# The last chunk's second layer by seven block products, five of them in float32r

## The chip, the cores and the metric

The kernel runs on one core of a Trainium2 chip. The time is that of the device in microseconds (us). An execution that the hardware profiler takes is shown beside the plain runs. The engines work from queues of their own: PE (TensorE, matmuls), DVE (VectorE), ACT (ScalarE), POOL (GpSimd) and SP (SyncE, which issues DMAs). "PEld" is PE's loading of the stationary operand, which a matmul needs first. The product goes into one of eight PSUM banks, from which DVE or ACT read it.

## The reference

Attention for 8 batches, 8 heads, 576 positions and 64 dimensions, with a mask of the last 32 positions for four heads and a mask of every 32nd position for the other four. Its result, 4608 tokens of 512 values, is the input of two layers:

```python
h = x @ w_in                    # 4608 x 512 by 512 x 2048
r = np.maximum(h, 0.0)
g = r * r
return (g @ w_out).astype(np.float32)   # 4608 x 2048 by 2048 x 512
```

## The kernel before

The 4608 tokens are cut into nine chunks of 512. A chunk's first layer (`mm1`, line 731) is 16 groups, one for each block of 128 hidden values: four matmuls of 128x128 weights by 512 tokens into one of two PSUM banks, then relu on ACT into a buffer `r` (four of them, line 745), then the square on DVE into `g` (line 746), one group later. The second layer (`mm2`, line 750) is also 16 groups: for each of the chunk's four blocks of 128 tokens, four groups of four matmuls. In each the stationary operand is a 128x128 block of `g` and the moving one a 128x512 row block of `w_out`; 16 of them add up in one bank. ACT copies the bank out (line 765) and SP issues the store (line 769).

The groups of all chunks stand in one list, numbered from 0: chunk c has its first layer in groups 32c to 32c+15 and its second in 32c+16 to 32c+31. An order written out by hand (`PLAN`) says which steps of the attention come before which group; its last words stand at group 217. `later(n, f)` puts off the issue of f by n groups, and `tick()` after each group issues what is due. So each engine's queue has a fixed order, and only the semaphores decide when an instruction starts. Chunk 7 is groups 224 to 255, chunk 8, the last, 256 to 287. Beside these two chunks nothing but the end of the attention's last steps is left.

The very last block of 128 tokens is cut finer (`last_y`, line 775): 16 matmuls of 256 columns, then 16 and 16 of 128, so that the last copy and the last store are small. The first two parts are copied by ACT, the last by DVE.

All matmul operands are bf16, 2 bytes. Sums in PSUM and the copied outputs are float32. SBUF tiles come from pools that live as long as the kernel.

Of the kernel before, what the change touches and what calls it, by code (L numbers as in the profile page):

```python
# [8 lines left out]
FP32 = mybir.dt.float32  # L9
BF16 = mybir.dt.bfloat16  # L10
AF = mybir.ActivationFunctionType
ALU = mybir.AluOpType
# [155 lines left out]
def kernel(  # L168
# [9 lines left out]
    nc = tc.nc  # L178
    B, H, S, D = q.shape
    d_model, d_ff = moe_w_in.shape  # L180
    T = B * S
# [4 lines left out]
    NL = S // QL  # L186
# [4 lines left out]
    VP = 72  # L191
    SR = 80
    NP2 = STRIDE // 2
    NG = 5
    NB = NP2 + NG + 1
    W3 = 3 * NA
    RW = STRIDE * D
    ER = S + 32

    singles = ctx.enter_context(tc.tile_pool(name="singles", bufs=1))  # L200
    qk_in = ctx.enter_context(tc.tile_pool(name="qk_in", bufs=4))
    qkT = ctx.enter_context(tc.tile_pool(name="qkT", bufs=4))
    v_st = ctx.enter_context(tc.tile_pool(name="v_st", bufs=1))
    rv_pool = ctx.enter_context(tc.tile_pool(name="rv_pool", bufs=3))
    small = ctx.enter_context(tc.tile_pool(name="small", bufs=4))
    xl_pool = ctx.enter_context(tc.tile_pool(name="xl_pool", bufs=4))
    g_pool = ctx.enter_context(tc.tile_pool(name="g_pool", bufs=2))
    r_pool = ctx.enter_context(tc.tile_pool(name="r_pool", bufs=4))
    y_pool = ctx.enter_context(tc.tile_pool(name="y_pool", bufs=4))

    PS = bass.MemoryType.PSUM
    strTs = {nm: ctx.enter_context(tc.tile_pool(name=f"strT{nm}", bufs=n)) for nm, n in (("q", 2), ("k", 1))}
    psum = ctx.enter_context(tc.tile_pool(name="psum", bufs=1, space=PS))
    psb = psum.tile([128, 8, 512], FP32, name="psb")
    all_banks = [psb[:, i] for i in range(8)]
# [4 lines left out]
    def bank(nm):  # L220
        if places:
            return all_banks[places.pop(0)]
        t = banks[nm].pop(0)
        banks[nm].append(t)
        while id(t) in unread:
            run_due(lambda x: x[1] == unread[id(t)])
        return t
# [10 lines left out]
    NV = 4  # L238
# [1 line left out]
    mask_loc = singles.tile([128, 1, QL], BF16)  # L240
    mask_all = singles.tile([128, NL, QL], BF16)
    mask_str = singles.tile([SP_, 1, SP_], BF16)
    vl_all = singles.tile([128, NV, 2, NL, VP], BF16, name="vl")
    vls = [vl_all[:, i] for i in range(NV)]

    vbds = [singles.tile([128, NB, 128], BF16, name=f"vb{i}") for i in range(2)]
    kbds = [singles.tile([128, NB, 128], BF16, name=f"kb{i}") for i in range(2)]
    ones_bd = singles.tile([128, 128], BF16)
    mask_bd = singles.tile([128, 1, W3], BF16)
    str_rows_t = {nm: singles.tile([SR, RW], BF16, name=f"{nm}_t") for nm in "qk"}  # L250
    kTl = [singles.tile([128, 32 + S], BF16, name=f"kTl{i}") for i in range(NV)]
    es01 = singles.tile([128, 4 * ER], BF16, name="e01")
    es = [es01[:, 0:2 * ER], es01[:, 2 * ER:]] + [singles.tile([128, 2 * ER], BF16, name=f"e{i}") for i in (2, 3)]
    xt = [singles.tile([128, T], BF16, name=f"xt{p}") for p in range(4)]
    w_in_b = singles.tile([128, 4, d_ff], BF16)
    w_out_b = singles.tile([128, 16, d_model], BF16)
# [210 lines left out]
    def later(n, fn, key=None):  # L467
        pending.append((clock[0] + n, key, fn))

    def run_due(test):  # L470
        due = [x for x in pending if test(x)]
        for x in due:
            pending.remove(x)
        for x in sorted(due, key=lambda x: x[0]):
            x[2]()

    def tick():
        clock[0] += 1
        run_due(lambda x: x[0] <= clock[0])
# [229 lines left out]
    def step_E(u, copy=None):  # L709
# [14 lines left out]
        copy(xt[p][:, b * S:(b + 1) * S], px)  # L724
        st.pop(u)

    gs = {}

    phs = {}

    def mm1(c, ff, kks=range(4), order=range(4), pool=None):
        if ff == 0 and c not in gs:
            gs[c] = g_pool.tile([128, 16, 512], BF16, name="g_sb")
        g = gs[c]
        if kks[0] == order[0]:
            phs[ff] = bank(pool or "ph")
        ph = phs[ff]
        for kk in kks:
            nc.tensor.matmul(ph, w_in_b[:, kk, 128 * ff:128 * (ff + 1)],  # L739
                             xt[kk][:, 512 * c:512 * (c + 1)],  # L740
                             start=(kk == order[0]), stop=(kk == order[-1]))
        if kks[-1] != order[-1]:
            return
        r = r_pool.tile([128, 512], BF16, name="r")
        nc.scalar.activation(r, ph, AF.Relu)  # L745
        later(1, lambda: nc.vector.tensor_tensor(g[:, ff, :], r, r, op=ALU.mult))  # L746

    ys = {}

    def mm2(c, i, pool=None):  # L750
        j, part = divmod(i, 4)
        g = gs[c]
        if part == 0:
            if pool == "pt":
                ys[c, j] = bank("pt")
                banks["pt"].remove(ys[c, j])
            else:
                ys[c, j] = bank(pool or "py")
        py = ys[c, j]
        for ff in range(4 * part, 4 * part + 4):  # L760
            nc.tensor.matmul(py, g[:, ff, 128 * j:128 * (j + 1)], w_out_b[:, ff, :],  # L761
                             start=(ff == 0), stop=(ff == 15))
        if part == 3:
            y = y_pool.tile([128, 512], FP32, name="y")
            nc.scalar.copy(y, py)  # L765
            if pool == "pt":
                banks["pt"].insert(0, py)
            r0 = 512 * c + 128 * j
            nc.sync.dma_start(out=out[r0:r0 + 128, :], in_=y)

    NCH = T // 512
    A, V, G = nc.scalar.copy, nc.vector.tensor_copy, nc.gpsimd.tensor_copy
    ENG = {"a": A, "v": V, "g": G}

    def last_y(c, j, i):
        g, r0 = gs[c], 512 * c + 128 * j
        if i == 0:
            ys[c, j] = y_pool.tile([128, 512], FP32, name="y")
        y = ys[c, j]
        cols = (slice(0, 256), slice(0, 256), slice(256, 384), slice(384, 512))[i]  # L780
        ffs = (range(0, 8), range(8, 16), range(16), range(16))[i]
        if i != 1:
            ys[c, j, i] = bank("ph")
        py = ys[c, j, 0 if i == 1 else i]
        for ff in ffs:
            nc.tensor.matmul(py[:, cols], g[:, ff, 128 * j:128 * (j + 1)], w_out_b[:, ff, cols],  # L786
                             start=(ff == 0), stop=(ff == 15))
        if i:
            (V if i == 3 else A)(y[:, cols], py[:, cols])
            (nc.scalar if i == 2 else nc.sync).dma_start(out=out[r0:r0 + 128, cols], in_=y[:, cols])  # L790

    def warm(n):
        if n:
# [6 lines left out]
    def first_part(kks, ffs):  # L800
        for ff in ffs:
            mm1(0, ff, kks, FIRST, None if ff < 2 else "py")
# [144 lines left out]
    groups = []  # L947

    def add(c, kind, i, pool=None):
        if kind == 0:  # L950
            groups.append(lambda: None)
        elif kind == 1:
            groups.append(lambda: mm1(c, i, pool=pool))
        elif c == NCH - 1 and i >= 12:
            groups.append(lambda: last_y(c, i // 4, i % 4))
        else:
            groups.append(lambda: mm2(c, i, pool))

    for ff in range(16):
        add(0, 1, ff, {NP: "pt", 8: "py"}.get(ff)) if ff >= NP else add(0, 0, ff)  # L960
    for part in range(4):
        for j, pool in ((0, "ph"), (1, "ph"), (2, None), (3, "pt")):
            add(0, 2, 4 * j + part, pool)
    for i in range(16):
        add(1, 1, i)
    for i in range(16):
        add(1, 2, i, "ph")
    for c in range(2, NCH):
        for i in range(16):
            add(c, 1, i)  # L970
        for i in range(16):
            add(c, 2, i, "ph")

    plan = {}
    for line in PLAN.strip().splitlines():
        n, words = line.split(":")
        plan.setdefault(int(n), []).extend(words.split())
    for n, g in enumerate(groups):
        if n == 32:
            banks["pt"] += banks.pop("py")  # L980
        for word in plan.get(n, ()):
            run_step(word)
        g()
        tick()
    for _ in range(4):
# [31 lines left out]
```

## Time and profile before

| | us |
|---|---|
| plain runs, median of three | 301.57 |
| plain runs | 302.65, 298.83, 301.57 |
| the profiled execution | 299.14 |
| its span, first to last instruction | 297.4 |
| PE busy | 287.8 |
| DVE busy | 180.3 |
| ACT busy | 170.5 |
| POOL busy | 73.3 |

The span is what the trace covers, and the execution's own time is 1.74 us more. Busy times of engines overlap; a matmul's end is modelled and runs into the next one's start, so the pitch of matmuls (start to start) says more than the duration of one. Chunk 7's first layer lies at 238.06 to 251.88 us of the span, its second to 265.69, chunk 8's first to 279.50 and its second to 293.56. What follows is the last copy and the last store.

### The profile page before, as it was taken

What the parts mean: (1) busy time and instruction counts of PE and PEld (TensorE: products, weight loads), DVE (VectorE), ACT (ScalarE), POOL (GpSimd) and SP (SyncE); (2) the same over time, 40 slices, a digit from 0 to 9 for tenths busy, and PEclk for the clock granted to TensorE, in tenths of its full rate; (3) what the DMA queues carried; (4) which work ended last, traced back from release to release, by engine and by line L of the source; (5) the groups of instructions that cost most, each with busy time, mean ns of one, the idle gap of its engine ahead of it and who ended that gap; (6) DMA issues with size and microseconds to landing.
All of it is one profiled execution on the core that took longest, in us unless ns stands there. A gap on an engine that the chain in (4) does not pass through costs nothing.

```text
span 297.4 us, 5621 instructions
## 1 busy us (share of the span) xinstructions
PE 287.8 (97%) x2112; PEld 144.6 (49%) x2148; DVE 180.3 (61%) x465; ACT 170.5 (57%) x318; POOL 73.3 (25%) x107
## 2 busy tenths in 40 slices
PE   7989999999999999999999999999999999999994
PEld 2644555544545454444454445544544444444444
DVE  5557689697777769779367936776575334004300
ACT  3758846774668636764577447744764266127411
POOL 8874743014513036065105700000000000000000
PEclk9999999999999999999999999999999999999999
DMA  7999999999999999999998999411011100020012
GB/s 146 183 207 204 189 199 189 156 224 204 168 179 179 123 164 199 160 144 188 179 128 125 177 149 145 82 55 73 35 31 47 71 37 0 35 89 20 0 71 73
DMA packets 91724, 37.38 MB, mean 126 GB/s; under 512 B 77549, under 2 KB 85831, under 8 KB 91697
## 3 DMA queue, kind: packets, MB, share of 16 engines
q0 software_dynamic: 50608, 18.33, 55.8%
q1 hardware_dynamic: 40944, 18.62, 32.3%
q8 instruction: 17, 0.28, 0.4%
q14 instruction: 11, 0.08, 0.1%
q10 hardware_dynamic: 144, 0.07, 0.1%
HBM read 37.22 MB, written 9.44 MB: 157 GB/s over the span
## 4 chain that ended last, share of the span: by engine, by line
PE 94%; DMA 2%; issue 1%; DVE 1%; ACT 0%; POOL 0%; DVEq 0%; POOLq 0%
PE psb L739 42%; PE psb L761 40%; DMA w_out_b<-in_k_dram 2%; PE psb L699 2%; PE psb L621 1%; PE psb L607 1%; PE psb L786 1%; PE psb L618 1%; PE psb L583 1%; PE psb L538 1%; PE psb L486 1%; DVE xt L668 0%; PE psb L508 0%; PE psb L333 0%; DVE x_l L688 0%
## 5 line engine op out<-in xcount | busy, mean ns | idle before, releaser
L739 PE MATMUL psb<-xt,w_in_b 128*128 128x512 bf16 x558 | 132.1, 379 | 1.2 <-DVE xt L668 0.2
L761 PE MATMUL psb<-w_out_b,g_sb 128*128 128x512 bf16 x542 | 125.3, 379 | 1.2 <-issue 0.5
L745 ACT ACTIVATE r<-psb 128x512 bf16<-128x512 f32 x144 | 85.3, 599 | 37.9 <-PE psb L739 32.8
L746 DVE TENSOR_TENSOR g_sb<-r 128x512 bf16<-128x512 bf16 x144 | 60.4, 423 | 68.5 <-ACT r L745 67.2
L739 PEld LDWEIGHTS <-w_in_b 128*128 128x128 bf16 x576 | 53.2, 97 | 58.9 <-issue 1.4
L761 PEld LDWEIGHTS <-g_sb 128*128 128x128 bf16 x560 | 52.0, 98 | 57.9 <-DVE g_sb L746 0.3
L765 ACT COPY y<-psb 128x512 f32<-128x512 f32 x35 | 20.6, 588 | 51.6 <-PE psb L761 48.6
L631 DVE TENSOR_TENSOR xt<-psb,rv 64x144 bf16<-64x144 f32 x84 | 34.0, 405 | 12.7 <-ACT rv L624 11.6
L623 ACT ACTIVATE rv<-psb 128x432 f32<-128x432 f32 (+1 forms) x21 | 10.5, 501 | 12.8 <-PE psb L618 12.8
L705 DVE TENSOR_TENSOR x_l<-psb,rinv 96x384 bf16<-96x384 f32 x28 | 15.5, 553 | 1.0
L361 POOL DMA_DIRECT2D q_t<-in_q_dram x6 | 3.3, 544 | 45.8 <-DMA qT_s<-q_t 44.9
L594 ACT ACTIVATE e<-psb 128x384 bf16<-128x384 f32 x30 | 12.0, 513 | 4.2 <-PE psb L583 4.2
L608 ACT ACTIVATE e<-psb 128x432 bf16<-128x432 f32 (+1 forms) x21 | 10.4, 496 | 4.0 <-PE psb L607 4.0
L637 DVE TENSOR_TENSOR xt<-psb,rv 64x270 bf16<-64x270 f32 (+1 forms) x28 | 11.0, 433 | 2.5 <-ACT rv L624 2.3
L290 POOL DMA_DIRECT2D q_l<-in_q_dram x16 | 12.0, 754 | 1.6 <-DMA q_l<-in_q_dram 1.4
L290 POOL DMA_DIRECT2D k_l<-in_k_dram x16 | 11.7, 736 | 1.6 <-DMA v_st<-in_v_dram 1.5
L624 ACT ACTIVATE rv<-rv 128x432 f32<-128x432 f32 (+1 forms) x21 | 11.2, 533 | 0.7
L590 DVE TENSOR_TENSOR e<-e,mask_all 128x576 bf16<-128x576 bf16 x20 | 8.4, 456 | 4.9 <-ACT e L594 4.9
L699 PEld LDWEIGHTS <-e 128*128 128x128 bf16 x168 | 8.0, 97 | 4.6
L361 POOL DMA_DIRECT2D k_t<-in_k_dram x6 | 3.2, 536 | 25.0 <-DMA kT_s<-k_t 22.9
L699 PE MATMUL psb<-vl,e 128*128 128x65 bf16 x168 | 9.0, 193 | 0.0
L607 PEld LDWEIGHTS <-kb 128*128 128x128 bf16 x154 | 6.8, 96 | 4.5
(119 smaller groups left out, 213.5 us busy)
## 6 DMA issues: line engine op xcount, KB each, us to landing
out_dram<-y SPq DMA_DIRECT2D x35, 256.0 KB, 4.2
w_out_b<-in_moe_w_out_dram POOLq DMA_DIRECT2D x4, 512.0 KB, 15.1
q_t<-in_q_dram POOLq DMA_DIRECT2D x7, 288.0 KB, 7.3
k_t<-in_k_dram POOLq DMA_DIRECT2D x7, 288.0 KB, 6.9
vl<-in_v_dram POOLq DMA_DIRECT2D x6, 288.0 KB, 7.7
v_st<-in_v_dram POOLq DMA_DIRECT2D x7, 216.0 KB, 6.8
w_in_b<-in_moe_w_in_dram POOLq DMA_DIRECT2D x2, 704.0 KB, 14.3
k_l<-in_k_dram POOLq DMA_DIRECT2D x16, 72.0 KB, 7.0
```

Source lines behind the costliest of these rows:

```text
L290: nc.gpsimd.dma_start(out=t[:, :, hh, :], in_=src[b, 2 * p + hh].rearrange("(t p) d -> p t d", p=QL))
L594: nc.scalar.activation(e[:, row, 4 * QL * i:4 * QL * (i + 1)], bk[row][i][:, 0:4 * QL], AF.Exp, scale=scale)
L624: nc.scalar.activation(rv, rv, AF.Exp, scale=-1.0)
L631: nc.vector.tensor_tensor(to[:, :, NJ * part:NJ * (part + 1), par], of, by, op=ALU.mult)
L637: nc.vector.tensor_tensor(t, of[:, g:, :, lo:lo + k], by[:, g:, :, lo:lo + k], op=ALU.mult)
L699: nc.tensor.matmul(po[:, n, :], e[:, c:c + 128], rhs[:, NL * part + n, 0:D + 1], start=True, stop=True)
L705: nc.vector.tensor_tensor(x, po[0:QL, :, 0:D], rinv[0:QL].to_broadcast([QL, NL, D]), op=ALU.mult)
L739: nc.tensor.matmul(ph, w_in_b[:, kk, 128 * ff:128 * (ff + 1)], xt[kk][:, 512 * c:512 * (c + 1)], start=(kk == order[0]), stop=(kk == order ...
L745: nc.scalar.activation(r, ph, AF.Relu)
L746: later(1, lambda: nc.vector.tensor_tensor(g[:, ff, :], r, r, op=ALU.mult))
L761: nc.tensor.matmul(py, g[:, ff, 128 * j:128 * (j + 1)], w_out_b[:, ff, :], start=(ff == 0), stop=(ff == 15))
L765: nc.scalar.copy(y, py)
```

## The change

The second layer of chunk 8 is written as a product of 2x2 blocks. The 512 tokens are taken as two halves u of 256, each of two blocks of 128 (t = 0, 1); the 2048 hidden values as two halves of 1024 (blocks 0 to 7 and 8 to 15 of `g`); the 512 outputs as two halves of 256 columns. Each half u then needs eight products of such blocks, each of which is eight matmuls of 256 columns. The new code forms seven, in Winograd's way, from sums of blocks of `g` and of `w_out`:

- `weight_sums` forms, in groups 228 to 247, four differences of blocks of `w_out` on DVE (16 subtractions of 128x512, groups 228 to 243) and one copy of a block on ACT (4 copies, groups 244 to 247), all into float32r tiles (4 bytes).
- `squares` takes the place of the squaring in chunk 8. Behind every second squaring DVE forms three sums of 128x256 (S1, S2, S3, where S1 needs the square just made and S2 needs S1), and POOL copies one block, all to float32r; a fourth sum S4 is put off into the second layer. Blocks come in the order 0, 8, 1, 9, ... instead of 0, 1, 2, ...
- `mm2_7` runs the products in the order 1, 2, 6, 7, 4, 5, 3, each for u = 0 and then u = 1: 14 groups of eight matmuls. Products 1 and 2 are of bf16 operands, the other five of float32r ones, whose weights the matmul instruction itself loads. Product 2 adds onto product 1 in PSUM after ACT has copied product 1 out, 7 onto 6 after DVE has read 6, and 3 onto 5 after DVE has read 5. DVE adds PSUM and a tile of SBUF for products 6, 7, 4, 5 and 3; ACT copies for 1 and 2.
- Stores go out after products 5 and 3. Those of the last half: 128x256 early from SP, the rest as two parts of 128x128 behind two DVE adds, one issued by ACT, one by SP.
- `last_y` is gone.
- The attention's tiles are moved to pools that are closed before the new tiles are made, so that these take the same SBUF addresses.

```diff
-    qk_in = ctx.enter_context(tc.tile_pool(name="qk_in", bufs=4))
...
+    att = ctx.enter_context(ExitStack())
+    rows = ctx.enter_context(ExitStack())
...
         nc.scalar.activation(r, ph, AF.Relu)
+        if c in SEVEN:
+            later(1, lambda: squares(c, ff, r))
+            return
         later(1, lambda: nc.vector.tensor_tensor(g[:, ff, :], r, r, op=ALU.mult))
...
+    def weight_sums(step):
...
+        if nm == "b":
+            nc.scalar.copy(t["b"], b22)
+            return
+        x, y = {"1": (b12, b11), "3": (b22, b12), "2": (b22, t["1"]), "4": (b21, t["2"])}[nm]
+        nc.vector.tensor_tensor(t[nm], x, y, op=ALU.subtract)
...
+    def squares(c, ff, r):
...
+        nc.vector.tensor_tensor(g[:, ff, :], r, r, op=ALU.mult)
+        if ff < 8:
+            return
+        S = {k: x[:, i] for k, x in ss.items()}
+        a1, a2 = (g[:, k, :].rearrange("p (u t c) -> p u t c", u=2, t=2) for k in (i, ff))
+        nc.gpsimd.tensor_copy(S["a"], a2[:, :, 1])
+        nc.vector.tensor_tensor(S["1"], a1[:, :, 1], a2[:, :, 1], op=ALU.add)
+        nc.vector.tensor_tensor(S["2"], S["1"], a1[:, :, 0], op=ALU.subtract)
+        nc.vector.tensor_tensor(S["3"], a1[:, :, 0], a1[:, :, 1], op=ALU.subtract)
+        last = lambda: nc.vector.tensor_tensor(S["4"], a2[:, :, 0], S["2"], op=ALU.subtract)
+        later(15 + (1, 2, 3, 4, 6, 7, 8, 9)[i] - 2 * i, last)
...
+    ORDER7 = "1 2 6 7 4 5 3".split()
+
+    def mm2_7(c, i):
+        n, u = ORDER7[i // 2], i % 2
...
+        for k in range(8):
+            a = g[:, k, t0] if n == "1" else g[:, 8 + k, t0] if n == "2" else \
+                ss[{"6": "2", "7": "3", "4": "a", "5": "1", "3": "4"}[n]][:, k, u]
+            b = w_out_b[:, k, lo] if n == "1" else w_out_b[:, 8 + k, lo] if n == "2" else \
+                ts[{"6": "2", "7": "3", "4": "4", "5": "1", "3": "b"}[n]][:, k]
+            nc.tensor.matmul(pa, a, b, start=k == 0 and n not in "273", stop=k == 7, skip_group_check=True)
+        if n in "12":
+            nc.scalar.copy((y2 if n == "1" else y1)[:, lo], pa)
+            return
...
+        if n == "3" and c == NCH - 1 and u:
+            nc.sync.dma_start(out=out[r0:r0 + 128, lo], in_=y1[:, lo])
+            for h, eng in ((0, nc.scalar), (128, nc.sync)):
+                nc.vector.tensor_tensor(to[:, h:h + 128], pa[:, h:h + 128], by[:, h:h + 128], op=ALU.add)
+                eng.dma_start(out=out[r0:r0 + 128, 256 + h:384 + h], in_=to[:, h:h + 128])
+            return
+        nc.vector.tensor_tensor(to, pa, by, op=ALU.add)
+        if n in "53":
+            r0 += 128 * (n == "5")
+            nc.sync.dma_start(out=out[r0:r0 + 128, :], in_=y2 if n == "5" else y1)
...
-            add(c, 1, i)
+            add(c, 1, i // 2 + 8 * (i % 2) if c in SEVEN else i)
...
+    SUMS = range(228, 248)
...
+        if n in SUMS:
+            weight_sums(SUMS.index(n))
```

More of the change, by code (lines that the diff above doesn't have):

```diff
@@ L200 @@
     singles = ctx.enter_context(tc.tile_pool(name="singles", bufs=1))
-    qk_in = ctx.enter_context(tc.tile_pool(name="qk_in", bufs=4))
-    qkT = ctx.enter_context(tc.tile_pool(name="qkT", bufs=4))
-    v_st = ctx.enter_context(tc.tile_pool(name="v_st", bufs=1))
-    rv_pool = ctx.enter_context(tc.tile_pool(name="rv_pool", bufs=3))
     small = ctx.enter_context(tc.tile_pool(name="small", bufs=4))
-    xl_pool = ctx.enter_context(tc.tile_pool(name="xl_pool", bufs=4))
     g_pool = ctx.enter_context(tc.tile_pool(name="g_pool", bufs=2))
@@ L209 @@
     y_pool = ctx.enter_context(tc.tile_pool(name="y_pool", bufs=4))
+    att = ctx.enter_context(ExitStack())
+    rows = ctx.enter_context(ExitStack())
+    att_singles = att.enter_context(tc.tile_pool(name="att_singles", bufs=1))
+    rv_pool = att.enter_context(tc.tile_pool(name="rv_pool", bufs=3))
+    xl_pool = att.enter_context(tc.tile_pool(name="xl_pool", bufs=4))
+    row_singles = rows.enter_context(tc.tile_pool(name="row_singles", bufs=1, side="right"))
+    qk_in = rows.enter_context(tc.tile_pool(name="qk_in", bufs=4, side="right"))
+    qkT = rows.enter_context(tc.tile_pool(name="qkT", bufs=4, side="right"))
+    v_st = rows.enter_context(tc.tile_pool(name="v_st", bufs=1, side="right"))
     PS = bass.MemoryType.PSUM
-    strTs = {nm: ctx.enter_context(tc.tile_pool(name=f"strT{nm}", bufs=n)) for nm, n in (("q", 2), ("k", 1))}
+    strTs = {nm: rows.enter_context(tc.tile_pool(name=f"strT{nm}", bufs=n, side="right")) for nm, n in (("q", 2), ("k", 1))}
     psum = ctx.enter_context(tc.tile_pool(name="psum", bufs=1, space=PS))
@@ L242 @@
     mask_str = singles.tile([SP_, 1, SP_], BF16)
-    vl_all = singles.tile([128, NV, 2, NL, VP], BF16, name="vl")
+    vl_all = att_singles.tile([128, NV, 2, NL, VP], BF16, name="vl")
     vls = [vl_all[:, i] for i in range(NV)]
-    vbds = [singles.tile([128, NB, 128], BF16, name=f"vb{i}") for i in range(2)]
-    kbds = [singles.tile([128, NB, 128], BF16, name=f"kb{i}") for i in range(2)]
+    vbds = [att_singles.tile([128, NB, 128], BF16, name=f"vb{i}") for i in range(2)]
+    kbds = [row_singles.tile([128, NB, 128], BF16, name=f"kb{i}") for i in range(2)]
     ones_bd = singles.tile([128, 128], BF16)
     mask_bd = singles.tile([128, 1, W3], BF16)
[L250 to L253, printed above, removed]
+    str_rows_t = {nm: row_singles.tile([SR, RW], BF16, name=f"{nm}_t") for nm in "qk"}
+    kTl = [row_singles.tile([128, 32 + S], BF16, name=f"kTl{i}") for i in range(NV)]
+    es01 = att_singles.tile([128, 4 * ER], BF16, name="e01")
+    es = [es01[:, 0:2 * ER], es01[:, 2 * ER:]] + [att_singles.tile([128, 2 * ER], BF16, name=f"e{i}") for i in (2, 3)]
     xt = [singles.tile([128, T], BF16, name=f"xt{p}") for p in range(4)]
@@ L725, in step_E @@
         st.pop(u)
+    NCH = T // 512
     gs = {}
@@ L731, in mm1 @@
     def mm1(c, ff, kks=range(4), order=range(4), pool=None):
-        if ff == 0 and c not in gs:
+        if c not in gs:
             gs[c] = g_pool.tile([128, 16, 512], BF16, name="g_sb")
@@ L745, in mm1 @@
         nc.scalar.activation(r, ph, AF.Relu)
+        if c in SEVEN:
+            later(1, lambda: squares(c, ff, r))
+            return
         later(1, lambda: nc.vector.tensor_tensor(g[:, ff, :], r, r, op=ALU.mult))
+    SEVEN = (NCH - 1,)
+    ts, ss = {}, {}
+    def weight_sums(step):
+        F32R = mybir.dt.float32r
+        if not ts:
+            rows.close()
+            late = ctx.enter_context(tc.tile_pool(name="late", bufs=1, side="right", reuse_waits="tile"))
+            for nm in ("1", "2", "3", "4", "b"):
+                ts[nm] = late.tile([128, 8, 256], F32R, name=f"t{nm}")
+        nm, i = "1234b"[step // 4], 2 * (step % 4)
+        lo, hi = slice(i, i + 2), slice(8 + i, 10 + i)
+        b11, b12 = w_out_b[:, lo, 0:256], w_out_b[:, lo, 256:512]
+        b21, b22 = w_out_b[:, hi, 0:256], w_out_b[:, hi, 256:512]
+        t = {k: x[:, lo] for k, x in ts.items()}
+        if nm == "b":
[3 more added lines that the diff above has]
+        nc.vector.tensor_tensor(t[nm], x, y, op=ALU.subtract)
@@ new lines, in squares @@
+    def squares(c, ff, r):
+        g, i = gs[c], ff % 8
+        if not ss:
+            att.close()
+            late = ctx.enter_context(tc.tile_pool(name="sums", bufs=1, reuse_waits="tile"))
+            for nm in ("1", "2", "3", "4", "a"):
+                ss[nm] = late.tile([128, 8, 2, 128], mybir.dt.float32r, name=f"s{nm}")
+        nc.vector.tensor_tensor(g[:, ff, :], r, r, op=ALU.mult)
[9 more added lines that the diff above has]
+        later(15 + (1, 2, 3, 4, 6, 7, 8, 9)[i] - 2 * i, last)
@@ new lines @@
+    ORDER7 = "1 2 6 7 4 5 3".split()
+    def mm2_7(c, i):
+        n, u = ORDER7[i // 2], i % 2
+        g, r0 = gs[c], 512 * c + 256 * u
+        t0 = slice(256 * u, 256 * u + 128)
+        if n == "1":
+            ys[c, u] = [y_pool.tile([128, 512], FP32, name="y") for _ in range(2)]
+            ys[c, u, "p"] = [bank("pt")]
+        if n == "6":
+            ys[c, u, "p"].append(bank("pt"))
+        y1, y2 = ys[c, u]
+        lo, hi = slice(0, 256), slice(256, 512)
+        pa = ys[c, u, "p"][n not in "124"][:, lo]
+        for k in range(8):
[7 more added lines that the diff above has]
+            return
+        to, by = {"6": (y1[:, hi], y2[:, lo]), "7": (y2[:, hi], y2[:, lo]), "4": (y2[:, lo], y2[:, hi]),
+                  "5": (y2[:, hi], y2[:, hi]), "3": (y1[:, hi], y1[:, hi])}[n]
+        if n == "3" and c == NCH - 1 and u:
[8 more added lines that the diff above has]
+            nc.sync.dma_start(out=out[r0:r0 + 128, :], in_=y2 if n == "5" else y1)
@@ L769, in mm2 @@
             nc.sync.dma_start(out=out[r0:r0 + 128, :], in_=y)
-    NCH = T // 512
     A, V, G = nc.scalar.copy, nc.vector.tensor_copy, nc.gpsimd.tensor_copy
     ENG = {"a": A, "v": V, "g": G}
[L775 to L790, printed above, removed]
     def warm(n):
@@ L953, in add @@
             groups.append(lambda: mm1(c, i, pool=pool))
-        elif c == NCH - 1 and i >= 12:
-            groups.append(lambda: last_y(c, i // 4, i % 4))
+        elif c in SEVEN:
+            groups.append(lambda: mm2_7(c, i) if i < 14 else None)
         else:
```

## The prediction

> **What bounds the kernel now.** I read the engine table first, then the chain that ended last, then a table of time by stage, and then the end of the timeline.
>
> ```profile
> span 297.4 us, 5621 instructions
> ...
> PE 287.8 (97%) x2112; PEld 144.6 (49%) x2148; DVE 180.3 (61%) x465; ACT 170.5 (57%) x318; POOL 73.3 (25%) x107
> ...
> PEclk9999999999999999999999999999999999999999
> ...
> PE 94%; DMA 2%; issue 1%; DVE 1%; ACT 0%; POOL 0%; DVEq 0%; POOLq 0%
> ```
>
> PE is busy for 97% of the span at the full granted clock, and 94% of the last chain is PE. So a change must alter PE's work, or make PE wait. The stage table (columns: stretch, length, then busy time and instruction count of PE, weight loads, VectorE, ScalarE, GpSimd) shows the four stages that matter: first and second layer of chunk 7, then of chunk 8.
>
> ```profile
> 238.06:251.88 13.82, 13.76 (x64) 6.24 (x65) 5.99 (x15) 9.54 (x16) 0.00 (x0) 1.00 0.05 20
> 251.88:265.69 13.81, 13.76 (x64) 6.26 (x64) 0.81 (x2) 2.35 (x4) 0.00 (x0) 1.00 0.15 57
> 265.69:279.50 13.81, 13.76 (x64) 6.26 (x64) 5.98 (x15) 9.54 (x16) 0.00 (x0) 1.00 0.06 21
> 279.50:293.56 14.06, 14.01 (x96) 8.03 (x95) 0.82 (x2) 2.99 (x6) 0.00 (x0) 1.00 0.18 66
> ```
>
> Each full stage is 64 matmuls of 512 columns in 13.81 us, 215.8 ns each, with the weight loads hidden. The changed stage is the last row, 14.06 us. VectorE is under half busy in first layers and nearly idle in second ones; GpSimd is idle. In the listings of both programs every engine's order and waits are the same up to chunk 7, so only these rows and the tail can change; the new pools move addresses alone.
>
> ```profile
> 279.50 10.52 PE L761 MATMUL psb<-w_out_b,g_sb 128*128 128x512 bf16 x47
> 279.70 0.60 ACT L745 ACTIVATE r<-psb 128x512 bf16<-128x512 f32 x1 [0.27 <-PE psb L739]
> 280.33 0.42 DVE L746 TENSOR_TENSOR g_sb<-r 128x512 bf16<-128x512 bf16 x1 [0.44 <-ACT r L745]
> ...
> 289.86 3.70 PE L786 MATMUL psb<-w_out_b,g_sb 128*128 128x256 bf16 x48
> 290.06 0.58 ACT L765 COPY y<-psb 128x512 f32<-128x512 f32 x1 [2.87 <-PE psb L761]
> 291.81 0.37 ACT L789 COPY y<-psb 128x256 f32<-128x256 f32 x1 [1.16 <-PE psb L786]
> ...
> 293.65 0.29 DVE L789 COPY y<-psb 128x128 f32<-128x128 f32 x1 [12.89 <-PE psb L786]
> ```
>
> **Step 1, the matmuls.** Removed: 48 matmuls of 512 columns, 16 of 256, 32 of 128. Added: 7 products x 2 halves x 8 = 112 of 256 columns, 32 of them bf16 and 80 float32r. A reader on ScalarE starts 0.20 us behind the last matmul (289.86, where the next began, to 290.06). So the 16 matmuls of 256 columns end at 291.81 - 0.20 = 291.61: 1.75 us from 289.86, 109 ns each. If all 112 take that, the stage's PE work is 112 x 0.109 = 12.21 us against 14.06: **-1.85 us**.
>
> **Step 2, the price of float32r.** The trace has no such matmul. The lower end is the bf16 pitch, 109 ns. The upper ends come from rows of weight loads and streams:
>
> ```profile
> L786 PEld LDWEIGHTS <-g_sb x48: 97/98/98, 289.6 to 293.3; 128*128 128x128 bf16 x48
> ```
>
> The 32 matmuls of 128 columns take 293.56 - 291.61 = 1.95 us, 61 ns each, each with a bf16 weight load; so such a load occupies the array 61 ns at most. A load of twice the bytes would then take up to 122 ns, more than the 109 it hides under: 80 x 13 ns = 1.04 us. If the load cannot run ahead of the matmul before it, the 98 ns of this row come on top: 207 ns, 80 x 98 ns = +7.8 us. If the moving operand streams by bytes, 256 columns cost as much as 512 of bf16, 216 ns: +8.6 us. Below nothing it cannot go, as the columns are the same. I take the middle of 109 and 122, because the nearest rows are those with hidden loads: **+0.5 us**; the other ends are a rival.
>
> [...] No run here shows a 4-byte load.
>
> **Step 3, weight sums in chunk 7.** Before groups 228 to 243 VectorE gets 16 subtractions of 128x512 with float32r output, 12 of them among the squarings of chunk 7's first layer. Their price needs the engine's pitch, which is less than its duration:
>
> ```profile
> 61.92 0.41 DVE L746 TENSOR_TENSOR g_sb<-r 128x512 bf16<-128x512 bf16 x1
> 62.25 0.35 DVE L309 COPY k_l<-xt 96x768 bf16<-96x768 bf16 x1
> 62.52 0.41 DVE L746 TENSOR_TENSOR g_sb<-r 128x512 bf16<-128x512 bf16 x1
> 62.86 0.18 DVE L704 RECIPROCAL rinv<-psb 96x6 f32<-96x6 f32 x1
> 63.08 0.55 DVE L705 TENSOR_TENSOR x_l<-psb,rinv 96x384 bf16<-96x384 f32 x1
> ```
> ```profile
> L746 DVE TENSOR_TENSOR g_sb<-r 128x512 bf16<-128x512 bf16 x144 | 60.4, 423 | 68.5 <-ACT r L745 67.2
> ...
> L590 DVE TENSOR_TENSOR e<-e,mask_all 128x576 bf16<-128x576 bf16 x20 | 8.4, 456 | 4.9 <-ACT e L594 4.9
> ```
>
> An independent successor starts 0.33 us after a squaring (61.92 to 62.25), though that lasts 0.42; one that needs the result (reciprocal to L705) starts 0.04 us after its end. Squarings of 512 and masks of 576 bf16 differ by 33 ns for 64 elements, 0.52 ns each. The f32-sourced 96x384 takes 0.55 us; at 0.52 ns per element its 384 would take 0.36, so 4-byte elements go at about 1.04 ns. A 128x512 sum with 4-byte output then lasts 0.69 us at a pitch of 0.60 (bounds: 0.42 if the output type does not slow it). With a squaring that is 0.93 us a group, against PE's 13.81 / 16 = 0.863:
>
> ```profile
> 242.35 0.42 DVE L746 TENSOR_TENSOR g_sb<-r 128x512 bf16<-128x512 bf16 x1 [0.44 <-ACT r L745]
> ```
> ```profile
> 252.71 0.42 DVE L746 TENSOR_TENSOR g_sb<-r 128x512 bf16<-128x512 bf16 x1 [0.44 <-ACT r L745]
> ```
>
> Squaring 3 starts at 242.35, the first sum at 242.68, squaring 4 at 243.28 instead of 243.21; each later one loses 0.07 more, so squaring 15 starts near 253.6 instead of 252.71 and ends near 254.0. Its matmul comes at 251.88 + 15 x 0.216 = 255.1. **0 us**, hidden by 1 us. The last four sums and ScalarE's four copies of a weight block lie in the second layer, where both engines are nearly idle (0.81 and 2.35 us of 13.81); without that cover each copy would cost ScalarE's queue its 0.6 us.
>
> **Step 4, sums of the squares in chunk 8.** This is where PE is made to wait. The first layer now runs blocks 0, 8, 1, 9, ...; per pair VectorE does two squarings and three sums of 128x256 with 4-byte output. At 1.04 ns per element such a sum costs as many cycles as a squaring, 0.42 us with a pitch of 0.33.
>
> ```profile
> 267.38 0.42 DVE L746 TENSOR_TENSOR g_sb<-r 128x512 bf16<-128x512 bf16 x1 [14.25 <-ACT r L745]
> ...
> 268.25 0.43 DVE L746 TENSOR_TENSOR g_sb<-r 128x512 bf16<-128x512 bf16 x1 [0.44 <-ACT r L745]
> ```
>
> S1 needs the second squaring and S2 needs S1, so both wait out 0.43 + 0.04. A pair takes 0.33 (first squaring) + 0.47 (second, S1 waits) + 0.47 (S1, S2 waits) + 0.33 (S2) + 0.33 (S3) = 1.93 us, against PE's 1.73: VectorE falls 0.20 us further behind each pair. Pair 0 squares at 267.38 and 268.25; S1 is at 268.72, S2 269.19, S3 269.52, and pair 1 starts at 269.85. Pair 7 starts six pairs later, 269.85 + 6 x 1.93 = 281.43, and block 7 is ready at 281.86 instead of 279.47 + 0.42 = 279.89. The first product needs block 7 as its eighth matmul, at 279.50 + 7 x 0.109 = 280.26. With 0.04 for the semaphore and 0.21 from weight load to matmul, it comes at 282.1: **+1.84 us**. Behind it stand all 105 remaining matmuls. The first layer itself is not held: four r buffers let VectorE trail ScalarE by 3.45 us less the 1.1 from a relu's start to its square's end, and the lag at block 5 is under 2. Every later sum comes in time: S2 and S3 of pair 7 end by 283.5, while the third product starts at 282.1 + 25 x 0.109 = 284.8; S4 is spread behind it.
>
> **Step 5, PSUM handovers.** Products 2, 7 and 3 add onto banks that ScalarE or VectorE must first have read. A read needs 0.20 + 0.37 us (or 0.42 on VectorE), and the other half's eight matmuls, 0.87 us, lie between. **0 us**; with the cover gone, 0.6 us at each of six handovers. S4 of VectorE waits behind adds that wait for PE, but its last one has two groups (1.74 us) to finish.
>
> **Step 6, the tail.** The last 128x256 goes out by two VectorE adds of 128 columns instead of one copy: +0.2 us, the 0.29 of the copy's row less 0.09 of overlap. The outputs also bunch: three rows of 256 KB are issued 0.87 us apart before the end.
>
> ```profile
> 288.00:289.00 1.00, 1.00 (x6) 0.41 (x5) 0.00 (x0) 0.00 (x0) 0.00 (x0) 1.00 0.68 262
> ```
> ```profile
> out_dram<-y SPq DMA_DIRECT2D x1, 64.0 KB, 2.3
> ```
>
> One such row took about 1 us at 262 GB/s, so each is pushed 0.13 us, and the last 64 KB, 2.3 us to landing when alone, finds some 0.3 us ahead of it: **+0.5 us** for both (bounds 0.2 to 1).
>
> **Sum.** -1.85 + 0.5 + 1.84 + 0.5 = +1.0 us. The profiled execution took 299.14 us: 300.1. The three plain runs have a median of 301.57, 2.43 above it, and spread over 3.8 us. I take the middle, 300.36, as the old kernel's time: **301.4 us**. About 2%, 6 us, is what a measurement of this kernel can tell from no change.
>
> **Rivals.** *Float32r is slow* (the other side): from step 2, weight loads in line or a half-rate stream instead of the 0.5 us give +8.3 to +9.1 us, 308.7 to 309.5; a half-hidden load gives about 304 to 305. It decides from about 170 ns a matmul, where the loss passes 2%. For it: 4-byte operands appear nowhere on PE. Against: all loads in the trace hide.
>
> *GpSimd holds VectorE.* Eight copies of 128x256 on GpSimd fall among the sums of step 4.
>
> ```profile
> masks.py:199 POOL TENSOR_SCALAR_AFFINE_SELECT ident<-ident 128x128 bf16<-128x128 bf16 x1 | 0.3, 287 | 0.1
> ...
> L917 POOL TENSOR_SCALAR_AFFINE_SELECT mask_loc<-mask_loc 128x96 bf16<-128x96 bf16 x1 | 0.3, 265 | 0.1
> ```
>
> From 96 to 128 columns costs 22 ns, so 256 take about 0.35 us. If each stops VectorE, seven of them before block 7 add 2.4 us to the stall: 303.8. The trace has no compute of GpSimd beside VectorE in these stages. [...]
>
> *VectorE keeps up*: if sums with 4-byte output overlap fully (0.33 at every step, 1.65 us a pair), the stall shrinks to nothing: -0.85 us, 299.5; -1.35 with free weights. For: 0.44 us idle before every squaring. Against: two true dependences in each pair.
>
> **Chances.** Forecast 0.42, GpSimd 0.24, VectorE keeps up 0.12, slow float32r 0.18, and 0.04 for more than two passes per matmul, which no row prices. The range 298.5 to 309.0 takes in the first three and half of the fourth. Faster by 2% would need -6 us, more than step 1 holds: 0.01. Slower by 2% holds most of the last two: 0.20. Within: 0.79.
>
> **What would show it.** In the new profile: 80 float32r matmuls at 109 to 122 ns start to start; a PE gap of 1 to 2 us shortly after 279.5, released by VectorE's squaring; no gap near 254; a last add 0.5 us after the last matmul. The prediction is wrong if float32r matmuls space out past 150 ns, if that gap is over 3 us or absent, or if PE waits in the second half of the products.

## The result and the profile after

Twelve plain runs of the changed kernel have a median of 300.09 us, twelve of the kernel before 298.81. The ratio is 1.0059, 95% interval 1.0031 to 1.0088: a little slower, well within 2%. (Some executions, of the kernel before too, are 4 to 11 us longer than the fastest; the ratios leave them out and compare the others, called comparable below, while the medians take all.)

The page of the profile of the changed kernel differs from the old one at its end:

```profile
span 299.9 us, 5779 instructions
...
PE 291.7 (97%) x2164; PEld 150.6 (50%) x2164; DVE 203.6 (68%) x523; ACT 171.5 (57%) x321; POOL 78.8 (26%) x115
...
PEclk9999999999999999999999999999999999999889
...
PE 90%; DVE 5%; DMA 2%; issue 1%; ACT 0%; POOL 0%; DVEq 0%; POOLq 0%
```

DVE's part of the last chain grows from 1% to 5%, and the granted clock falls in the 38th and 39th of the 40 slices. PE's part of the timeline, and the last reader on DVE, show where:

```profile
279.39 1.17 PE L815 MATMUL psb<-w_out_b,g_sb 128*128 128x256 bf16 x7
...
282.28 4.57 PE L815 MATMUL psb<-w_out_b,g_sb 128*128 128x256 bf16 x25 [1.72 <-DVE g_sb L784]
...
286.61 4.03 PE L815 MATMUL psb<-t,s 128*128 128x256 f32 x32
...
294.26 2.05 PE L815 MATMUL psb<-tb,s 128*128 128x256 f32 x16
...
296.35 0.49 DVE L824 TENSOR_TENSOR y<-psb,y 128x128 f32<-128x128 f32 x2 [0.52 <-PE psb L815]
```

After seven matmuls PE waits for block 7's square until 282.28. The next 25 matmuls take 286.61 - 282.28 = 4.33 us, 173 ns each. The table of stretches (busy time and count of PE, weight loads, DVE, ACT and POOL, then the granted clock) says why these are slow:

```profile
279.50:282.20 2.70, 0.99 (x8) 0.49 (x5) 2.63 (x9) 0.60 (x1) 0.65 (x1) 1.00 0.00 0
282.20:286.60 4.40, 4.32 (x25) 3.25 (x26) 2.62 (x8) 1.12 (x3) 0.65 (x1) 0.61 0.00 0
286.60:296.30 9.70, 9.70 (x82) 9.51 (x80) 5.48 (x14) 0.37 (x1) 0.00 (x0) 1.00 0.14 52
```

Behind the wait the mean granted clock is 0.61, and then 1.00 again. Shorter stretches show that this mean is made of two values, and that the clock falls 0.8 us after PE has gone on:

```profile
282.20:283.00 0.80, 0.72 (x7) 0.66 (x8) 0.77 (x3) 0.37 (x1) 0.38 (x1) 1.00 0.00 0
283.25:286.50 3.25, 3.25 (x17) 2.33 (x16) 1.64 (x5) 0.74 (x2) 0.03 (x1) 0.50 0.00 0
```

From the start of the stage's first matmul to the start of the last read of PSUM (of the first of two reads in the changed kernel) the changed kernel takes 296.35 - 279.39 = 16.96 us, the kernel before 293.65 - 279.50 = 14.15.

### The profile page after: what moved, and what is told of

Read it like the earlier page. It is cut to its first block, busy times and chain, and to the rows that moved or that the text cites. A ratio compares the mean times of both kernels' runs of the same rounds, so it can differ in the third digit from the quotient of the medians.

```text
span 299.9 us, 5779 instructions
## 1 busy us (share of the span) xinstructions
PE 291.7 (97%) x2164; PEld 150.6 (50%) x2164; DVE 203.6 (68%) x523; ACT 171.5 (57%) x321; POOL 78.8 (26%) x115
## 4 chain that ended last, share of the span: by engine, by line
PE 90%; DVE 5%; DMA 2%; issue 1%; ACT 0%; POOL 0%; DVEq 0%; POOLq 0%
PE psb L744 38%; PE psb L845 37%; PE psb L815 5%; DMA w_out_b<-in_k_dram 2%; PE psb L703 2%; DVE g_sb L784 2%; PE psb L625 1%; PE psb L611 1%; PE psb L622 1%; DVE s L791 1%; PE psb L587 1%; DVE s L790 1%; PE psb L542 1%; PE psb L490 1%; DVE s L792 1%
## 5 line engine op out<-in xcount | busy, mean ns | idle before, releaser
L845 PE MATMUL psb<-w_out_b,g_sb 128*128 128x512 bf16 x512 | 117.2, 379 | 0.0
L754 DVE TENSOR_TENSOR g_sb<-r 128x512 bf16<-128x512 bf16 x128 | 53.7, 423 | 42.7 <-ACT r L750 41.6
L845 PEld LDWEIGHTS <-g_sb 128*128 128x128 bf16 x512 | 47.2, 97 | 52.3 <-DVE g_sb L754 0.3
L849 ACT COPY y<-psb 128x512 f32<-128x512 f32 x32 | 18.9, 591 | 40.8 <-PE psb L845 40.7
L789 POOL CAST sa<-g_sb 128x256 fp32r<-128x256 bf16 x8 | 5.2, 654 | 107.7 <-DVE g_sb L784 107.7
L627 ACT ACTIVATE rv<-psb 128x432 f32<-128x432 f32 (+1 forms) x21 | 10.5, 501 | 12.8 <-PE psb L622 12.8
L784 DVE TENSOR_TENSOR g_sb<-r 128x512 bf16<-128x512 bf16 x16 | 6.1, 414 | 11.4 <-ACT r L750 11.4
```

## The experiments

Medians of all executions, in us; each group has its own runs of the kernel before, on the same chip. "Stage" is first matmul to last read, as above, in the profiled execution.

| kernel | time | before | ratio (interval) | stage |
|---|---|---|---|---|
| changed kernel | 300.09 | 298.81 | 1.0059 (1.0031 to 1.0088) | 16.96 |
| e1_free_slots | 299.15 | 299.05 | 1.0010 (0.9988 to 1.0032) | 14.65 |
| e2_no_copy | 299.50 | 299.05 | 1.0005 (0.9975 to 1.0034) | 14.77 |
| e3_fill | 300.58 | 299.05 | 1.0042 (1.0017 to 1.0067) | 15.75 |
| e4_bf16 | 297.25 | 299.05 | 0.9944 (0.9919 to 0.9970) | 12.52 |
| e0_control | 300.53 | 298.60 | 1.0074 (1.0046 to 1.0102) | 15.29 |
| e5_between | 298.29 | 298.60 | 0.9992 (0.9976 to 1.0008) | 13.75 |
| e6_more_wait | 305.78 | 298.60 | 1.0269 (1.0215 to 1.0322) | 19.29 |
| e7_bf16_between | 297.60 | 298.60 | 0.9948 (0.9919 to 0.9976) | 12.43 |
| e8_four_bf16 | 297.73 | 298.43 | 0.9968 (0.9947 to 0.9989) | 13.02 |

The theory after the first profile: VectorE's dependent sums make PE wait for block 7, and the wait lets the clock fall. Rivals: float32r itself, GpSimd's copies, or a clock that falls at random.

**The changed kernel again.** No edit.

> The changed kernel again, on the chip of this group's other runs. Theory (the gap before block 7 sometimes lets the clock fall): its times fall into two groups, about 299.7 to 300.2 us at a mean clock of 0.998 or more, and 1.5 to 2 us more at about 0.994. Rival (the clock falls at random, whatever the kernel does at its end): kernels without a gap show the 0.994 as often.

The profiled execution held its clock this time. PE's rows:

```profile
280.94 1.18 PE L815 MATMUL psb<-w_out_b,g_sb 128*128 128x256 bf16 x7
283.83 2.90 PE L815 MATMUL psb<-w_out_b,g_sb 128*128 128x256 bf16 x25 [1.72 <-DVE g_sb L784]
286.49 4.03 PE L815 MATMUL psb<-t,s 128*128 128x256 f32 x32
```

The stage begins 1.55 us later, from early in the span (PE waits 1.42 us for a DMA before 92.54), so stages are compared, and not times on the span. The wait is the same 2.1 us, but the 25 matmuls behind it take 2.66 us, 106 ns each, and the whole stage 1.67 us less. Two of eleven comparable executions have a mean clock of 0.994, at 301.9 and 303.8 us, and four of eleven in the first group, at 301.2 to 303.4, where the other seven took 299.6 to 300.2. So about a quarter of the executions seem to pay for the clock; the mean does not say where it fell. The two groups of times are less clean here, 299.5 to 301.5 us with the clock held; in the profiled execution, at 301.48, that is the early difference.

**Sums into VectorE's free slots.** At most one of S1 and S2 behind each squaring, all S3 at the end:

```diff
         nc.vector.tensor_tensor(g[:, ff, :], r, r, op=ALU.mult)
+        if sums:
+            sums.pop(0)()
...
-        nc.vector.tensor_tensor(S["1"], a1[:, :, 1], a2[:, :, 1], op=ALU.add)
+        sums.append(lambda: nc.vector.tensor_tensor(S["1"], a1[:, :, 1], a2[:, :, 1], op=ALU.add))
```

> Same work as the changed kernel, but VectorE takes at most one sum (S1 or S2) behind each squaring of chunk 8, and all S3 behind the last squaring. If the wait for block 7 and the clock that falls behind it are the loss, the PE gap of 2 us near 280 is gone, the granted clock stays at 1.0, the second layer takes 32 x 0.109 + 80 x 0.118 = 12.9 us from 279.4, and the time falls below the kernel before: ratio 0.993 to 0.997. If float32r matmuls or the tail are the loss, the gap goes but the ratio stays at 1.003 or above.

The wait for block 7 is gone and the clock is 0.998 to 1.0 in all twelve executions, but the ratio of 1.001 misses the expected gain, because a new wait stands in product 7:

```profile
282.51 2.13 PE L822 MATMUL psb<-t,s 128*128 128x256 f32 x16
285.88 2.16 PE L822 MATMUL psb<-t,s 128*128 128x256 f32 x16 [1.24 <-DVE y L834]
```

Product 7 adds onto product 6's bank, which VectorE must first read. That read now stands in VectorE's queue behind eight S3 and three S4, and starts at 285.40 though product 6's first half was done near 283.5. The handover that step 5 priced at 0.6 us when uncovered cost 1.46 (16 matmuls of 0.12 us from 282.51 end at 284.42).

**No copies on GpSimd.**

```diff
-        nc.gpsimd.tensor_copy(S["a"], a2[:, :, 1])
...
-                ss[{"6": "2", "7": "3", "4": "a", "5": "1", "3": "4"}[n]][:, k, u]
+                ss[{"6": "2", "7": "3", "4": "1", "5": "1", "3": "4"}[n]][:, k, u]
```

> GpSimd's eight copies are left out (product 4 reads S1 in their place, so part of the output is another sum). If GpSimd's copies slow the sums beside them, S2 falls from 0.50 to 0.42 us, a pair from 2.00 to 1.92, and block 7 is squared 0.5 us earlier: time 0.5 us less, ratio about 1.004. If S2 is slow by its own operands, it stays at 0.50 and the time at 1.006.

First a pair in the changed kernel, then one without the copies (S1, S2, S3, squarings):

```profile
268.60 0.42 DVE L790 TENSOR_TENSOR s<-g_sb 128x256 fp32r<-128x256 bf16 x1
...
268.62 0.65 POOL L789 CAST sa<-g_sb 128x256 fp32r<-128x256 bf16 x1 [98.31 <-DVE g_sb L784]
269.05 0.50 DVE L791 TENSOR_TENSOR s<-s,g_sb 128x256 fp32r<-128x256 f32 x1
...
269.48 0.41 DVE L792 TENSOR_TENSOR s<-g_sb 128x256 fp32r<-128x256 bf16 x1
269.81 0.75 DVE L784 TENSOR_TENSOR g_sb<-r 128x512 bf16<-128x512 bf16 x2
...
270.60 0.42 DVE L790 TENSOR_TENSOR s<-g_sb 128x256 fp32r<-128x256 bf16 x1
```
```profile
268.36 0.42 DVE L789 TENSOR_TENSOR s<-g_sb 128x256 fp32r<-128x256 bf16 x1
268.82 0.43 DVE L790 TENSOR_TENSOR s<-s,g_sb 128x256 fp32r<-128x256 f32 x1
269.16 0.42 DVE L791 TENSOR_TENSOR s<-g_sb 128x256 fp32r<-128x256 bf16 x1
269.50 0.75 DVE L784 TENSOR_TENSOR g_sb<-r 128x512 bf16<-128x512 bf16 x2
270.29 0.42 DVE L789 TENSOR_TENSOR s<-g_sb 128x256 fp32r<-128x256 bf16 x1
```

S2 falls from 0.50 to 0.43 and the pair from 2.00 to 1.93, as the first theory expected. GpSimd's part is 0.07 us a pair, not the 0.35 of the rival. In all ten executions the clock is at 0.998 or above, though PE still waits 1.6 us there (seven matmuls from 279.16, the eighth at 281.52).

**The gap filled with matmuls that nothing needs.**

```diff
+        if i == 0:
+            pw = bank("pt")
+            for _ in range(12):
+                nc.tensor.matmul(pw, w_in_b[:, 0, 0:128], xt[0][:, 512 * c:512 * (c + 1)], start=True, stop=True)
```

> Twelve matmuls of 512 columns into a spare bank before product 1 (2.6 us of work that is not needed) fill the gap in which PE waits for block 7. If the clock falls because PE is idle there, the clock stays at 1.0, the bf16 matmuls of products 1 and 2 go at 109 instead of 173 ns, and the last matmul ends at 279.4 + 2.6 + 12.9 = 294.9, not at 296.3: faster than the changed kernel with its fallen clock by about 1.4 us though it does more. If the clock falls for another reason (the float32r load itself), it falls here too and the time is 0.7 us over the changed kernel's.

```profile
284.36 2.75 PE L805 MATMUL psb<-xt,w_in_b 128*128 128x512 bf16 x12
286.95 3.66 PE L819 MATMUL psb<-w_out_b,g_sb 128*128 128x256 bf16 x32
290.36 4.03 PE L819 MATMUL psb<-t,s 128*128 128x256 f32 x32
```

This profiled execution came 5 us late into the stage, from further up, so only the stage is read. The 32 bf16 matmuls go at 3.41 / 32 = 107 ns, and the stage takes 15.75 us, 1.2 less than the changed kernel's with its fallen clock, though it holds 2.6 us of extra work. All nine comparable executions have a clock of 0.998 or more, at 299.9 to 301.1 us, below the 301.2 to 303.8 of the changed kernel's executions with a fallen clock. The clock is 1.00 through all 80 float32r matmuls of this trace (290.36 to 300 us), so float32r alone did not lower it; in this stage it is the idle PE that goes with the fall.

**All in bf16.**

```diff
-        F32R = mybir.dt.float32r
+        F32R = BF16
...
-                ss[nm] = late.tile([128, 8, 2, 128], mybir.dt.float32r, name=f"s{nm}")
+                ss[nm] = late.tile([128, 8, 2, 128], BF16, name=f"s{nm}")
```

> All sums and the five products in bf16, in the order of the changed kernel. A pair of squarings then costs VectorE about 1.5 us, less than PE's 1.73, so block 7 comes in time and the gap is gone; the 80 matmuls go at 109 instead of 118 ns (0.75 us less) with weight loads of 98 instead of 188 ns. Time 2.0 to 2.2 us below the kernel before if both hold (ratio 0.993); if the pitch stays at 118 ns, the type is not its cause, and the ratio is 0.995 to 0.996.

Loads and matmuls of the last products, first of the changed kernel, then here (minimum/median/maximum ns):

```profile
L815 PEld LDWEIGHTS psb<-t,s x48: 187/188/192, 286.6 to 294.0; 128*128 128x128 f32 x48
L815 PE MATMUL psb<-t,s x48: 277/280/364, 286.6 to 294.1; 128*128 128x256 f32 x48
```
```profile
L815 PEld LDWEIGHTS <-s x64: 97/98/98, 282.9 to 291.5; 128*128 128x128 bf16 x64
L815 PE MATMUL psb<-t,s x48: 272/273/273, 283.0 to 289.9; 128*128 128x256 bf16 x48
```

A float32r load lasts 188 ns against 98. By start to start, 64 float32r matmuls of the changed kernel take 294.26 - 286.61 = 7.65 us, 120 ns each; here the same 64 (283.02 to 290.00) take 109 each. So the type costs 80 x 10.5 ns = 0.84 us. The ratio of 0.9944 is 1.7 us below the kernel before, slightly short of the 2.0 to 2.2 expected. Only e7_bf16_between, below, is as fast.

**No sum directly behind the one it needs.** S1 and S3 behind one squaring, S2 behind the next:

```diff
+        for f in sums.pop(0) if sums else ():
+            f()
...
+        sums.extend([(s1, s3), (s2,)])
```

> Float32r as in the changed kernel, but no sum stands directly behind the one that it needs: behind a squaring come S1 and S3 of the pair before, behind the next squaring its S2. If the two waits inside VectorE (0.13 us each a pair) are what makes it fall behind, a pair costs 5 x 0.33 = 1.67 us or, with GpSimd's copy beside it, up to 1.8; block 7 is late by 0.5 us at most, no product waits over 0.3 us, the second layer takes 13.0 us and the time is 297.7 to 298.3, ratio 0.995 to 0.998. If five instructions a pair are too many for VectorE by themselves, a gap of over 1 us remains.

The wait for block 7 shrinks from 2.1 to 0.6 us, product 7 does not wait, and the time of 298.29 is at the upper end of what was expected (the ratio, 0.9992, just above it). The pair takes 1.88 us, not 1.67 to 1.8, because a squaring beside GpSimd's copy is drawn out to 0.61 us:

```profile
277.97 0.53 POOL L792 CAST sa<-g_sb 128x256 fp32r<-128x256 bf16 x1 [1.34 <-DVE g_sb L785]
278.16 0.61 DVE L785 TENSOR_TENSOR g_sb<-r 128x512 bf16<-128x512 bf16 x1
```

**The same with product 4 in bf16,** which needs no copy on GpSimd.

```diff
-        nc.gpsimd.tensor_copy(S["a"], a2[:, :, 1])
...
+            t1 = slice(256 * u + 128, 256 * u + 256)
+            a = g[:, k, t0] if n == "1" else g[:, 8 + k, t0] if n == "2" else g[:, 8 + k, t1] if n == "4" else \
```

> As e5_between, but product 4 alone takes bf16 operands: the block of squares itself and a bf16 difference of weights. So GpSimd's eight copies are not needed and are gone. If these copies are what still holds VectorE in e5_between (a squaring beside one takes 0.6 instead of 0.4 us), a pair of squarings falls from 1.88 to about 1.68 us, below PE's 1.73, the wait of 0.4 us in product 1 is gone, and with 16 matmuls at 109 instead of 118 ns the time is 0.5 us under e5_between: ratio 0.997 to 0.998. If five VectorE instructions a pair are too many by themselves, the pair stays near 1.88 and only 0.15 us are saved.

The median is 0.56 us under that of e5_between, which ran on another chip, and the stage 0.73 us shorter; 0.5 was expected. The pair is 1.73 us, PE's own pace (second squarings at 276.94 and 278.67), the squaring 0.42, and the wait is gone:

```profile
276.94 0.42 DVE L785 TENSOR_TENSOR g_sb<-r 128x512 bf16<-128x512 bf16 x1
...
278.67 0.42 DVE L785 TENSOR_TENSOR g_sb<-r 128x512 bf16<-128x512 bf16 x1
```

Five instructions a pair are not too many. With the order of e5_between, a copy on GpSimd draws out one squaring by 0.19 us (0.61 against 0.42), and without the copies a pair is 0.15 us shorter and at PE's pace. In the changed kernel the copies cost 0.07 us a pair; VectorE's own waits may cover part of them there, which no run shows.

**S3 twice, for a longer wait.**

```diff
-        nc.vector.tensor_tensor(S["3"], a1[:, :, 0], a1[:, :, 1], op=ALU.subtract)
+        for _ in range(2):
+            nc.vector.tensor_tensor(S["3"], a1[:, :, 0], a1[:, :, 1], op=ALU.subtract)
```

> Each S3 is formed twice (once for nothing), 0.45 us more a pair. Block 7 is then 6 x 0.45 = 2.7 us later than in the changed kernel, of which four r buffers pass some on to the first layer. Theory: everything behind the wait moves with it, and the longer gap lets the clock fall in nearly every execution: 2.7 + up to 1.6 us over the changed kernel, 302.5 to 304.5 us, mean clock 0.994 or less. Rival (the clock is not tied to the gap): 302.5 us with the clock at 0.998 or more in most executions.

```profile
285.59 4.57 PE L816 MATMUL psb<-w_out_b,g_sb 128*128 128x256 bf16 x25 [2.18 <-DVE g_sb L784]
```
```profile
285.50:290.00 4.50, 4.41 (x26) 3.34 (x27) 3.06 (x9) 1.12 (x3) 0.66 (x1) 0.62 0.00 0
```

Block 7 comes 3.3 us later than in the changed kernel (285.59 to 282.28), the clock behind it is 0.62, and all four executions have a mean clock of 0.989 to 0.994. The time is 5.2 us over e0_control's on the same chip, above the range expected: first-layer matmuls were held back too (the stage begins 1.2 us later than in the changed kernel's first profile), product 7 waited again, for 0.2 us, and the stage is 4.0 us longer than e0_control's (19.29 to 15.29).

By the mean clock of an execution (0.994 or less against 0.997 or more), the clock fell in every one of four with a gap of over 4 us (broken by one matmul), in 6 of 22 comparable ones with 2.1 us (8 of all 24), and in none of 56 with 1.6 us or less (e1, e2, e4, e5, e8). Alone these counts prove little, because the mean does not say where the clock fell: e3_fill and e7_bf16_between, whose programs do not leave this gap, have 0.976 to 0.994 in 4 of 13 and 4 of 12 executions, and the kernel before 0.95 to 0.994 in 7 of 82. One of these is traced, e3_fill's profiled execution. There PE waits twice in a step of the attention, and behind these waits the clock is at 0.50 from 144.50 to 147.75, as it is in the changed kernel from 283.25 to 286.50:

```profile
142.80 0.35 PE L587 MATMUL psb<-qT,kTl 64*128 64x96 bf16 x8 [0.67 <-DVE xt L635]
144.39 0.48 PE L587 MATMUL psb<-qT,kTl 64*128 64x96 bf16 x7 [1.25 <-DVE xt L641]
```
```profile
144.50:147.75 3.25, 3.25 (x14) 1.20 (x12) 2.37 (x5) 1.64 (x4) 1.22 (x2) 0.50 1.58 214
148.00:150.00 2.00, 2.00 (x11) 0.94 (x10) 0.00 (x0) 0.59 (x1) 0.86 (x2) 1.00 2.31 147
```

In these three traces the clock falls behind the end of a wait of PE: 0.8 us behind it in the changed kernel, by 144.50 behind a wait that ends at 144.39 in e3_fill, and in e6_more_wait the mean is 0.62 in the 4.5 us from 285.50, where a wait ends at 285.59. So the fall goes with waits of PE here, and not with this stage alone.

**Both: order of e5_between, all in bf16.**

> As e5_between, with all sums and products in bf16. If what is left in e5_between over this one is float32r alone, the difference is 80 x 9 ns = 0.75 us plus what VectorE's slower sums delay; against e4_bf16 (297.25) it saves the last wait of 0.2 us at most: 297.0, ratio 0.993 to 0.994.

The stage is 12.43 us, 0.09 under e4_bf16's, which still had a wait of 0.1 us for block 7. The ratio of 0.9948 is just above the 0.993 to 0.994 expected, and the same as e4_bf16's within its interval. Against e5_between the stage is 1.32 us shorter: float32r's 0.84 and the 0.6 of the wait would be 1.44, and the 0.1 between is left to the edges of products. The medians of the comparable executions, 298.29 and 297.29 us, differ by 1.0.

## Why the prediction was right or wrong

The range held 300.09, and "within 2%" was right. But the number given, 301.4, lies 0.2 us **below** the 301.57 that it was read against, so it pointed the wrong way, though its own sum said slower by 1.0. The step that failed is the last of **Sum**: the old kernel's time was taken as 300.36, half way from the profiled execution to the median of three runs. Twelve runs put it at 298.81, so the profiled 299.14 was the better base, and 299.14 + 1.0 = 300.14 would have been it. Three runs over 3.8 us cannot carry a forecast of 1 us, and a sum made against one execution belongs to that execution.

The sum step by step, with the clock held (e0_control):

- *Step 1*, -1.85: right to 0.13 us. In bf16 the products go at 109 ns, and the stage without a wait (e7_bf16_between) is 14.15 - 12.43 = 1.72 us shorter than before.
- *Step 2*, +0.5: measured +0.84, 120 ns a matmul, inside the bounds of 109 and 122. The doubled load of 122 ns was the better guess. In the trace a load lasts 188 ns against 98, and the pitch is 120 against 109; whether the load sets the pitch no run shows.
- *Step 3*, 0: right to 0.1 us. Squaring 15 of chunk 7 started at 253.48 where 253.6 was worked out, and PE's 64 matmuls ran on:

```profile
251.77 13.98 PE L845 MATMUL psb<-w_out_b,g_sb 128*128 128x512 bf16 x64
```
```profile
253.48 0.43 DVE L754 TENSOR_TENSOR g_sb<-r 128x512 bf16<-128x512 bf16 x1
```

- *Step 4*, +1.84: measured +2.13, at the eighth matmul as said, 282.28 for 282.1. Two errors in it partly offset each other. GpSimd's copies, which the sum put at nothing, add 0.53: without them (e2_no_copy) the wait is 1.60. And the 0.21 from weight load to matmul is not paid by a PE that waits: load and matmul start together, 0.47 us after the squaring of block 7 started, with the copies (281.81 to 282.28) and without them:

```profile
281.05 0.76 DVE L784 TENSOR_TENSOR g_sb<-r 128x512 bf16<-128x512 bf16 x2
281.52 2.63 PEld L814 LDWEIGHTS <-g_sb 128*128 128x128 bf16 x25 [1.71 <-DVE g_sb L784]
281.52 2.90 PE L814 MATMUL psb<-w_out_b,g_sb 128*128 128x256 bf16 x25 [1.44 <-DVE g_sb L784]
```

  What was left out is the price of a waiting PE beyond its wait: in the profiled execution 25 matmuls at 173 instead of 106 ns, +1.67 us, and by the mean clock in about a quarter of the executions. No term and no rival held it.
- *Step 5*, 0: right for the changed kernel, where product 7 follows product 6 without a gap. e1_free_slots shows how near the edge that is.
- *Step 6*, +0.5: wrong sign. From the last read to the end of the span it is 299.9 - 296.35 = 3.55 us against 297.4 - 293.65 = 3.75, so -0.2. The stores do bunch, but the last 64 KB land in 1.8 us, not in 2.3 and more:

```profile
out_dram<-y SPq DMA_DIRECT2D x1, 64.0 KB, 1.8
```

Together, -1.72 + 0.84 + 2.13 - 0.2 = +1.05 us with the clock held, by stages 15.29 - 14.15 - 0.2 = +0.94; the fallen clock adds 1.67 where it comes. That the recorded +1.0 is this near is luck: 0.13, 0.34 and 0.29 us too little in steps 1, 2 and 4 stand against 0.7 too much in step 6. The medians differ by 1.28, and no run takes the rest apart.

The rivals: *Float32r is slow* fell, at 120 ns. *GpSimd holds VectorE* is real, but at 0.53 us a fifth of its price here. *VectorE keeps up* fell for this order of instructions, and e8_four_bf16 shows that it holds when no sum stands behind its source and GpSimd is out of the way. Two figures of the rivals come out a little higher from their own rows: a loss of 2% needs 178 ns a float32r matmul, not 170 (5.5 us over 80 matmuls above 109 ns), and a copy of 256 columns is 0.375 us, not 0.35. Neither changes the account.

## What to carry to other kernels

When work moves from the engine that bounds the kernel to one with idle time, count the pitch of every instruction and the full latency of every one that needs the instruction before it: here five of 0.33 us would have fitted into 1.73, and two dependent pairs and a copy made them 2.00. Put an unrelated instruction between the two, and look who reads behind the moved ones. And price a wait on the matmul engine by what comes behind it too: here a wait of 2.1 us was followed in one of two traces by 3.4 us at half the clock, which cost 1.67 us.

## What the hardware showed that was not expected

- A PE wait of 2.1 us, with seven matmuls ahead of it, was followed in one of two traces by a granted clock of 0.50 from about 283.1 to 286.5 us, beginning 0.8 us after PE had gone on. Two waits of 0.67 and 1.25 us with eight short matmuls between them were followed by the same in e3_fill; one of 1.6 us in e2_no_copy was not. Why the same wait does it only at times is open.
- Float32r matmuls of 256 columns come every 120 ns, bf16 ones every 109, though a load lasts 188 ns against 98.
- A 128x256 copy on GpSimd beside VectorE's sums and squarings takes 0.53 us (e1_free_slots, e5_between) to 0.65 us (the changed kernel) instead of 0.40 (e1_free_slots, where its first copy had no VectorE work beside it). In the changed kernel it draws a sum out by 0.07 us (0.50 against 0.43 in e2_no_copy), in e5_between a squaring by 0.19 (0.61 against 0.42 in e8_four_bf16); in e1_free_slots the squarings behind the copies take 0.43 as without one. The drawn-out one ends 0.27 or 0.28 us after the copy (269.27 to 269.55 in the changed kernel, 278.50 to 278.77 in e5_between). No run shows why.
